# Zero matmuls in more of the early holes of the matrix engine, and exponentials of scores by one instruction a bank, in an attention and channel-mix kernel

## The chip, the core and the metric

The kernel runs on one core of a Trainium2 chip. Such a core has a matrix engine (TensorE, PE in the profile, with its weight loads as PEld), a vector engine (VectorE, DVE), a scalar engine for functions such as exp (ScalarE, ACT), a general engine (GpSimd, POOL) and an engine that issues transfers (SyncE, SP). Each works through its own instructions in order and waits for others by semaphores. TensorE writes its results into PSUM, eight banks of 512 float32 columns on 128 partitions. The metric is the device time in microseconds (us), smaller is better.

## What is computed

Attention with 32 memory slots for 8 batches of 8 heads, 576 tokens and 64 dimensions, then a channel mix of the RWKV kind (shift by one token, two projections, a squared ReLU, a gate):

```python
a = np.exp(phi - phi.max(2)); a = a / a.sum(2)
k_m, v_m = einsum('bhsm,bhsd->bhmd', a, k), einsum('bhsm,bhsd->bhmd', a, v)
attn = softmax(scale * q @ k_m.T)
x = (attn @ v_m), heads side by side: (8, 576, 512)
x_prev = x shifted by one token
xk, xr = mu_k * x + (1 - mu_k) * x_prev, mu_r * x + (1 - mu_r) * x_prev
k = np.maximum(xk @ w_k, 0); v = k * k @ w_v
out = sigmoid(xr @ w_r) * v
```

## The kernel before

The order of all work is written out by hand in `PLAN`, a list of words that is read once. A word `0:s0@0123` is a step of batch 0 (here the first part of its scores) that takes PSUM banks 0 to 3 for its results; `/a` and `/d` say which engine (ACT or DVE) does a step that either can do; `c0:6a` is a key product (the first part of the tokens for the seventh block of 128 columns of w_k), `g:` a gate, `o:` an output product, `r:` and `s:` ReLU and square, `p:` the issue of a load on POOL's queue, `b:8x8` eight matmuls on zeros of 8 x 64 = 512 columns. Since every engine keeps the order of its words, a word's place sets what it is queued behind.

Batches go through the same steps: exp of phi (line 298), sums over tokens (`z`, line 328) and products with k and v (`kg`, `vg`, `k`, `v`, `kv`, line 318), a transpose of the normalised k (`tk`, line 367), a transpose of q on DVE (`q0`, `q1`, lines 385 to 390), the scores (`s`, line 404), their exponentials on ACT (`es`, lines 420 and 425), the denominators, and the product of exponential and inverse denominator (`w`, in batch 0 `y`, line 466), which gives the attention weights.

Batch 0 goes its own way: denominators by matmul (`l`, line 432), logarithm and exponential on ACT (lines 437, 442), then `mk` and `mr` (line 361) mix tokens and values into x, `uk` and `ur` (line 547) copy it out as bf16, and the key products `c0:` (line 601) and gates (line 658) follow. The row mub (line 260) is a small product that spreads mu_k and mu_r. In batches 1 to 7 the values are folded into the weights first (`G`, line 493, copied out at line 499), and keys and gates are made from the attention weights (lines 619 to 679); their denominators come from DVE alone, which transposes the exponentials (`fe`, line 447), sums them (`fs`, line 453) and spreads the inverse (`fo`, line 459).

In batches 1 to 7 the tokens are kept with even ones before odd ones. The scores come out in another order, and the exponential writes them where they belong: for each of two halves of the batch (c) and two banks (w) four instructions (the four rows of `EVEN_ODD`, 5 or 4 blocks of 16 elements each, so 80 or 64 elements), 16 a batch. `weigh` then multiplies `e` and `lz` element by element into `at`, all three in the same order.

Matmuls on zeros: `keep_busy` writes into one tile, `idle`, in bank 7. `WARM` asks for 78 of 64 columns at the start; the words `b:` ask for 16 more, on 6720 columns, between `0:c10/a` and `0:s1@0123`, that is among the first steps of batch 0. `ps_tile` takes the next bank of a word, and its tile waits until the readers and writers of the tile that was there before are done; `covered` notes how many columns of a bank a tile has written.

Loads are issued by POOL in the order of the words `p:` (q, k, v, phi of later batches, and the weights wk, wr, wv), each waiting for earlier ones and for its buffer; phi and k of batch 0 are issued by ACT at the start.

Of the kernel before, what the change touches and what calls it, by code (L numbers as in the profile page):

```python
# [10 lines left out]
F32 = mybir.dt.float32  # L11
BF16 = mybir.dt.bfloat16
U32 = mybir.dt.uint32
AF = mybir.ActivationFunctionType
# [2 lines left out]


PLAN = [
# [71 lines left out]
NJ = 9  # L91
# [5 lines left out]
def kernel(  # L97
# [13 lines left out]
    nc = tc.nc  # L111
# [5 lines left out]
    scale = 1.0 / (D ** 0.5)  # L117
# [4 lines left out]
    PB = QR // 2  # L122
    HALVES = (slice(0, 5 * QR), slice(5 * QR, S))
    FIRST = (slice(0, 4 * QR), slice(4 * QR, S))
    CT = 512
# [11 lines left out]
    def ps_tile(shape, dtype, name, cover=0, onto=0):  # L137


        bank = next(now["banks"])  # L140
        if onto:
            assert covered.get(bank, 0) >= onto, (name, bank)
        else:
            covered[bank] = cover
        return psum.tile(shape, dtype, name=name, tag="ps" + bank, bufs=1)
# [31 lines left out]
    k0 = work.tile([128, HH, NJ, D], F32, name="k0f", tag="G", bufs=2)  # L177
# [55 lines left out]
    for g in range(4):  # L233
        r = slice(g * M, (g + 1) * M)
# [8 lines left out]
    xk_T, xr_T = x0_T[:, 0], x0_T[:, 1]  # L243
    sq = big.tile([128, NF, 2 * S], BF16, name="sq")

    idle = ps_tile([128, CT], F32, "idle")

    def keep_busy(n, blocks=CT // 64):
        for _ in range(n):
            ps = idle[:, :blocks * 64]  # L250
            nc.tensor.matmul(ps.rearrange("p (a b) -> p a b", b=64), lhsT=zeros,  # L251
                             rhs=zeros[:, :64].unsqueeze(1).to_broadcast([128, blocks, 64]), start=True, stop=True,
                             skip_group_check=True)

    keep_busy(*WARM)

    def load_mu_b():
# [9 lines left out]
    def load_mu():  # L267
# [2 lines left out]
        yield  # L270
        nc.vector.tensor_copy(mu1, ps_mu)

    EVEN_ODD = [(0, slice(0, 5), (0, slice(0, NJ, 2))), (0, slice(5, NJ), (1, slice(1, NJ, 2))),
                (1, slice(0, 4), (0, slice(1, NJ, 2))), (1, slice(4, NJ), (1, slice(0, NJ, 2)))]
    state = [{} for _ in range(B)]

    def scale_w(name):
# [11 lines left out]
    def attention(b):  # L289
        st = state[b]  # L290
# [119 lines left out]
        def exp_scores(c, js=slice(0, NJ)):  # L410

            def go():
                if "e" not in st:
                    st["e"] = work.tile([128, 2, S], BF16, name="e", tag="e", bufs=3)
                if b:
                    e = st["e"][:, c].rearrange("p (r v u) -> p r v u", r=2, u=PB)
                    for w in range(2):
                        ps = st["sc", 0][c, w].rearrange("p j (u r) -> p r j u", r=2)
                        for r, vs, js_ in EVEN_ODD:
                            nc.scalar.activation(e[:, r, vs, w * PB // 2:(w + 1) * PB // 2], ps[:, js_[0], js_[1]],  # L420
                                                 AF.Exp, scale=scale)
                    return
                e = st["e"][:, c].rearrange("p (j w t) -> p w j t", w=2, t=PB)
                for hf in range(2):
                    nc.scalar.activation(e[:, hf, js], st["sc", js.start][c, hf], AF.Exp, scale=scale)
            return go
# [35 lines left out]
        def weigh(c, sl=slice(0, S)):  # L462
            def go():
                if "at" not in st:
                    st["at"] = work.tile([128, 2, S], BF16, name="atn", tag="atn", bufs=3)
                nc.vector.tensor_mul(st["at"][:, c, sl], st["e"][:, c, sl], st["lz"][:, c, sl])  # L466
            return go

        def tr_v():
# [316 lines left out]
    for word in " ".join(PLAN).split():  # L786
        word, _, used = word.partition("@")
        word, _, now["by"] = word.partition("/")
        now["banks"] = iter(used)
        who, _, name = word.partition(":")  # L790
        if who == "p":
            preload(name)
        elif who == "b":
            keep_busy(*map(int, name.split("x")))
        else:
            queues[1:] = [nc.scalar] * (word in TAIL)
            parts = pending.pop(word, None) or (mixes[who][name] if who in mixes else attend[int(who)](name))()
            if hasattr(parts, "send") and next(parts, who) is not who:
                pending[word] = parts
# [31 lines left out]
```

## Time and profile before

| what | us |
|---|---|
| median of 3 runs (202.01 to 203.43) | 202.44 |
| the profiled execution's own time | 202.97 |
| its span, from the first instruction to the last | 201.0 |
| TensorE busy | 187.4 |
| VectorE busy | 158.8 |
| ScalarE busy | 152.3 |
| chain that ended last: TensorE, ScalarE, VectorE | 72%, 10%, 10% |

The profile is of one execution. Busy time of an engine is the union of its instructions. TensorE's matmuls overlap, and the end of each is modelled, so one of a group has a length that is longer than its share. In the rows of a timeline stand the start, the length, the engine, the line of the kernel, the operation, what it writes and reads, its shape, and the count of the instructions drawn together; in brackets the idle time of the engine before it and what ended it. "Clock" is the share of TensorE's full clock that was granted.

### The profile page before, as it was taken

Reading aid. Unit: us, or ns where it says so; the run is one execution under the profiler, and the core shown is the slowest. Engines: PE = TensorE matmul, PEld = TensorE weight load, DVE = VectorE, ACT = ScalarE, POOL = GpSimd, SP = SyncE. Lnnn points to the kernel's source line nnn. Section 1 sums busy time; section 2 is a strip of 40 time slices with the busy share of each in tenths; the row PEclk is TensorE's granted clock in tenths of the full one; section 3 lists DMA queues with packets and bytes.
Section 4 is the critical chain, followed back from the end, with each engine's and each line's share of the span. In section 5 each row is a group of like instructions: output and inputs, shape, how many; then the busy total and the mean of one; then the engine's idle time right before and its main releaser. Section 6 shows DMA issues by size and latency. Waiting matters only on the chain.

```text
span 201.0 us, 6598 instructions
## 1 busy us (share of the span) xinstructions
PE 187.4 (93%) x2650; PEld 106.4 (53%) x2650; DVE 158.8 (79%) x352; ACT 152.3 (76%) x434; POOL 29.3 (15%) x44
## 2 busy tenths in 40 slices
PE   8498798989999999999999999999999999999990
PEld 8334466548764455735655466346634564465440
DVE  2143479898887999999988999799979998999230
ACT  2427478988789688989899868998895799978310
POOL 7554320100170100502004200000000000000000
PEclk9999579999999999999999999999999999999997
DMA  5999999999999993599928999115102420123143
GB/s 195 278 203 265 206 208 199 253 220 283 225 171 214 208 308 120 94 231 287 293 74 126 213 248 245 31 40 137 36 3 65 118 82 10 47 76 86 33 124 104
DMA packets 26174, 31.95 MB, mean 159 GB/s; under 512 B 3096, under 2 KB 20768, under 8 KB 26144
## 3 DMA queue, kind: packets, MB, share of 16 engines
q0 software_dynamic: 17376, 20.32, 55.1%
q1 hardware_dynamic: 7408, 9.19, 15.9%
q10 hardware_dynamic: 1360, 2.03, 3.1%
q8 instruction: 20, 0.33, 0.6%
q14 instruction: 10, 0.08, 0.1%
HBM read 38.28 MB, written 9.44 MB: 237 GB/s over the span
## 4 chain that ended last, share of the span: by engine, by line
PE 72%; ACT 10%; DVE 10%; DMA 3%; issue 2%; ACTq 1%; DVEq 0%
PE pv L749 26%; PE pk L619 6%; PE pk L627 6%; PE pb L627 5%; PE gps L493 4%; PE pk L601 4%; PE kvps L318 3%; ACT e L420 3%; DMA k0f<-in_k_dram 3%; PE pr L679 3%; PE pr L671 2%; PE pb L679 2%; PE pv L743 2%; DVE rl L587 2%; ACT rl L585 2%; PE idle L251 2%
## 5 line engine op out<-in xcount | busy, mean ns | idle before, releaser
L749 PE MATMUL pv<-wv,sq 128*128 128x512 bf16 (+1 forms) x288 | 60.3, 356 | 0.3 <-DVE sq L593 0.2
L499 ACT CAST G<-gps 128x512 bf16<-128x512 f32 x75 | 40.5, 640 | 5.2 <-PE gps L493 4.9
L749 PEld LDWEIGHTS <-sq 128*128 128x128 bf16 x288 | 26.9, 97 | 29.3 <-issue 4.0
L755 DVE SCALAR_TENSOR_TENSOR o<-sg,pv 128x512 f32<-128x512 f32 (+3 forms) x41 | 24.4, 614 | 8.3 <-PE pv L749 5.0
L627 PEld LDWEIGHTS <-G 128*128 128x128 bf16 x224 | 21.3, 97 | 8.0 <-issue 1.0
L627 PE MATMUL pk<-diff,G 128*128 128x288 bf16 x112 | 22.9, 286 | 0.0
L627 PE MATMUL pb<-diff,G 128*128 128x288 bf16 x112 | 22.9, 286 | 0.0
L593 DVE TENSOR_TENSOR sq<-rl 128x576 bf16<-128x576 bf16 (+2 forms) x49 | 20.6, 438 | 1.8 <-ACT rl L585 0.7
L623 ACT COPY pb<-pk 128x288 f32<-128x288 f32 x43 | 16.6, 398 | 5.7 <-PE pk L619 4.0
L619 PE MATMUL pk<-atn,G 128*128 128x288 bf16 x112 | 20.3, 286 | 0.0
L585 ACT ACTIVATE rl<-pk 128x288 bf16<-128x288 f32 (+2 forms) x39 | 16.2, 419 | 3.8 <-PE pk L627 2.0
L648 ACT ACTIVATE sg<-pr 128x512 f32<-128x512 f32 x22 | 13.5, 624 | 7.2 <-PE pr L701 4.0
L585 ACT ACTIVATE rl<-pb 128x288 bf16<-128x288 f32 x36 | 14.7, 424 | 3.5 <-PE pb L627 3.3
L587 DVE TENSOR_SCALAR rl<-pk 128x288 bf16<-128x288 f32 (+2 forms) x33 | 14.5, 447 | 1.5 <-PE pk L601 1.0
L420 ACT ACTIVATE e<-scps 128x80 bf16<-128x80 f32 (+1 forms) x112 | 15.0, 320 | 0.1
L502 DVE TENSOR_TENSOR G<-G 128x1024 bf16<-128x1024 bf16 x21 | 14.1, 683 | 0.5 <-ACT G L499 0.4
L466 DVE TENSOR_TENSOR atn<-e,lz 128x576 bf16<-128x576 bf16 (+2 forms) x18 | 12.1, 688 | 3.0 <-ACT lz L442 2.8
L619 PEld LDWEIGHTS <-G 128*128 128x128 bf16 x112 | 10.6, 98 | 5.5
L591 ACT ACTIVATE sq<-rl 128x576 bf16<-128x576 bf16 (+2 forms) x23 | 12.4, 561 | 0.4 <-DVE rl L587 0.3
L298 ACT ACTIVATE em<-ph 128x1152 bf16<-128x1152 f32 (+1 forms) x9 | 9.8, 1083 | 1.8 <-DMA ph<-in_phi_dram 1.8
L601 PE MATMUL pk<-x0T,wk 128*128 128x256 bf16 (+1 forms) x64 | 10.9, 326 | 0.0
L251 PE MATMUL idle<-zeros 128*128 128x64 bf16 (+3 forms) x94 | 9.7, 280 | 1.0 <-DVE zeros L180 1.0
(100 smaller groups left out, 285.4 us busy)
## 6 DMA issues: line engine op xcount, KB each, us to landing
out_dram<-o SPq DMA_DIRECT2D x134, 64.0 KB, 3.5
ph<-in_phi_dram POOLq DMA_DIRECT2D x7, 576.0 KB, 10.3
kv<-in_k_dram POOLq DMA_DIRECT2D x7, 576.0 KB, 13.6
q<-in_q_dram POOLq DMA_DIRECT2D x7, 576.0 KB, 12.7
kv<-in_v_dram POOLq DMA_DIRECT2D x7, 576.0 KB, 13.1
k0f<-in_k_dram ACTq DMA_DIRECT2D x2, 576.0 KB, 6.9
wv<-in_moe_w_v_dram POOLq DMA_DIRECT2D x2, 512.0 KB, 19.1
ph<-in_phi_dram ACTq DMA_DIRECT2D x1, 576.0 KB, 4.6
```

Source lines behind the costliest of these rows:

```text
L420: nc.scalar.activation(e[:, r, vs, w * PB // 2:(w + 1) * PB // 2], ps[:, js_[0], js_[1]], AF.Exp, scale=scale)
L499: return lambda: copier()(g_tile()[:, v, c, GCOLS[i]], st["gps", v, i][c])
L502: return lambda: nc.vector.tensor_sub(g_tile()[:, 1, :, GCOLS[i]], g_tile()[:, 2, :, GCOLS[i]], g_tile()[:, 0, :, GCOLS[i]])
L585: nc.scalar.activation(rl, ps, AF.Relu, scale=HALF ** 0.5)
L587: nc.vector.tensor_scalar(rl, ps, 0.0, HALF ** 0.5, op0=AL.max, op1=AL.mult)
L593: nc.vector.tensor_mul(dst, rl, rl)
L601: nc.tensor.matmul(pk, lhsT=wk_sb[:, di, fi * 128:(fi + 1) * 128], rhs=xk_T[:, di, sl], start=(di == 0), stop=(di == ND - 1))
L619: nc.tensor.matmul(pa, lhsT=st["G"][:, 2, c, f], rhs=st["at"][:, c, :NP], start=c == 0, stop=False, skip_group_check=True)
L623: copier()(pb, pa)
L627: nc.tensor.matmul(ps, lhsT=st["G"][:, v, c, f], rhs=st["d"][:, kind, c], start=False, stop=c == 1, skip_group_check=True)
L749: nc.tensor.matmul(pv[:, cols], lhsT=sq[:, fi, lo:lo + 128], rhs=wv_sb[:, fi, cols], start=(fi == 0), stop=(fi == NF - 1))
L755: nc.vector.scalar_tensor_tensor(o[:, cols], in0=gated[name][:, cols], scalar=1.0, in1=pv[:, cols], op0=AL.add, op1=AL.mult)
```

## The change

There are two parts, and the rest of the order stays: without the words `b:`, the two plans are the same, word for word.

1. The words `b:` are now 42 matmuls on 18816 columns in place of 16 on 6720. They stand from the first exponential of phi to the key products of batch 0 (the last before `c0:2a`), most in bank 7, some in banks 3, 6 and 2. `keep_busy` takes a tile of its own for each word, in the bank that the word names, and so waits for that bank's last readers and writers. The 78 at the start stay.
2. The exponentials of batches 1 to 7 are one instruction for each bank, of 288 elements, that writes even and odd tokens of each block apart (4 a batch in place of 16); the order of blocks that `EVEN_ODD` made is now made by `weigh`, whose product reads `e` and `lz` in the order of blocks and writes `at` even before odd.

```diff
-    "0:exp0 0:c01/d 0:c00/a 0:exp1 0:z@0 0:z 0:mub@1 0:mub p:q:0h 0:kg0@02 0:c11/d 0:q1 0:c10/a b:8x8 b:1x2 0:kg1",
-    "0:h1/a 0:h0/a b:2x8 b:1x5 0:tk@0 0:q0 p:v:0h p:v:0g 0:tk b:1x8 b:1x4 0:s0@0123 0:es00 0:vg1@45 0:es10 b:1x3",
-    "0:l00@6 0:l00 b:1x3 0:s1@0123 0:l10@6 0:es11 p:wk:0-2 0:r00 0:y00 0:vg0 0:mu@2 0:mu 0:l10 0:l11@7 p:wk:4-8",
-    "0:es01 p:wk:2-4 0:l01@0 p:phi:1 0:nk0 0:nk1 0:r10 0:y10 0:l01 0:mk0@2130 0:l11 0:nr1 p:k:1 p:q:1 0:r01 0:r11",
+    "0:exp0 0:c01/d 0:c00/a 0:exp1 b:7x8@7 b:1x5@7 0:z@0 0:z 0:mub@1 0:mub p:q:0h 0:kg0@02 0:c11/d 0:q1 0:c10/a",
+    "b:10x8@7 0:kg1 0:h1/a 0:h0/a b:3x8@7 b:1x4@7 0:tk@0 0:q0 p:v:0h p:v:0g 0:tk b:2x8@7 0:s0@0123 0:es00 b:1x4@7",
+    "0:vg1@45 0:es10 b:1x7@7 0:l00@6 0:l00 b:1x6@7 0:s1@0123 b:1x4@7 0:l10@6 0:es11 p:wk:0-2 0:r00 0:y00 0:vg0",
+    "b:1x4@3 0:mu@2 0:mu 0:l10 0:l11@7 p:wk:4-8 0:es01 p:wk:2-4 b:1x8@3 b:1x8@6 0:l01@0 p:phi:1 0:nk0 0:nk1 0:r10",
+    "0:y10 0:l01 b:3x8@6 b:1x4@6 0:mk0@2130 0:l11 0:nr1 p:k:1 p:q:1 0:r01 0:r11 0:nr0 0:y01 0:y11 b:3x8@6 0:mk1@4576",
+    "0:uk01/a 0:uk00/a c0:6a@0 c0:5a@1 0:uk11/d 0:uk10/a 0:mr0@2347 0:ur01/d b:1x4@6 c0:6b@5 c0:3b@6 c0:4b@3 c0:0a@7",
...
+    "0:ur11/a p:wv:0-2 c0:5a/d b:1x4@6 1:z@6 c0:2b@7 c0:3b/d c0:0a/a b:1x4@2 c0:3a@4 c0:7a@5 c0:5b/d 0:tb c0:6a/a",
+    "0:ur10/d 1:k@12 c0:3a/a m:k0/d c0:5b/d b:1x4@3 c0:2a@3 1:z 1:nk/d c0:6a/a c0:1b@6 c0:7b@1 c0:3a/a c0:7b/a",
...
-    idle = ps_tile([128, CT], F32, "idle")
-
     def keep_busy(n, blocks=CT // 64):
+        ps = ps_tile([128, CT], F32, "idle", cover=blocks * 64)[:, :blocks * 64]
         for _ in range(n):
-            ps = idle[:, :blocks * 64]
             nc.tensor.matmul(ps.rearrange("p (a b) -> p a b", b=64), lhsT=zeros,
...
-                    e = st["e"][:, c].rearrange("p (r v u) -> p r v u", r=2, u=PB)
+                    e = st["e"][:, c].rearrange("p (h j u) -> p h j u", h=2, u=PB)
                     for w in range(2):
-                        ps = st["sc", 0][c, w].rearrange("p j (u r) -> p r j u", r=2)
-                        for r, vs, js_ in EVEN_ODD:
-                            nc.scalar.activation(e[:, r, vs, w * PB // 2:(w + 1) * PB // 2], ps[:, js_[0], js_[1]],
-                                                 AF.Exp, scale=scale)
+                        nc.scalar.activation(e[:, :, :, w * PB // 2:(w + 1) * PB // 2],
+                                             st["sc", 0][c, w].rearrange("p j (u h) -> p h j u", h=2), AF.Exp, scale=scale)
...
-                nc.vector.tensor_mul(st["at"][:, c, sl], st["e"][:, c, sl], st["lz"][:, c, sl])
+                out, e, z = st["at"][:, c, sl], st["e"][:, c, sl], st["lz"][:, c, sl]
+                if b:
+                    out = out.rearrange("p (r v u) -> p v r u", r=2, u=PB)
+                    e, z = (x.rearrange("p (v r u) -> p v r u", r=2, u=PB) for x in (e, z))
+                nc.vector.tensor_mul(out, e, z)
```

More of the change, by code (lines that the diff above doesn't have):

```diff
@@ L271, in load_mu @@
         nc.vector.tensor_copy(mu1, ps_mu)
-    EVEN_ODD = [(0, slice(0, 5), (0, slice(0, NJ, 2))), (0, slice(5, NJ), (1, slice(1, NJ, 2))),
-                (1, slice(0, 4), (0, slice(1, NJ, 2))), (1, slice(4, NJ), (1, slice(0, NJ, 2)))]
     state = [{} for _ in range(B)]
```

5 rows, old and new, of the table PLAN are left out of this document.

## The prediction

> **What bounds the kernel now.** I read the page first (whole span, then the 40 slices), then the clock by stretches, then TensorE's timeline, and last what the other engines and the loads do beside it.
>
> ```profile
> span 201.0 us, 6598 instructions
> PE 187.4 (93%) x2650; PEld 106.4 (53%) x2650; DVE 158.8 (79%) x352; ACT 152.3 (76%) x434; POOL 29.3 (15%) x44
> PE   8498798989999999999999999999999999999990
> PEclk9999579999999999999999999999999999999997
> ```
>
> TensorE (PE) is busy in nine tenths or more of every slice from about 40 us to the end: there the kernel is bound by TensorE. Only the first 40 us (eight slices) have holes and a lower clock. In stretches (us from the start, then busy time by engine, granted clock, DMA share, GB/s):
>
> ```profile
> 8.50:13.68 5.18, 5.18 (x53) 2.63 (x50) 2.85 (x8) 0.67 (x1) 2.23 (x3) 1.00 1.23 214
> 13.68:20.51 6.83, 5.75 (x212) 3.05 (x210) 2.30 (x9) 4.79 (x18) 3.26 (x4) 1.00 1.26 249
> 20.51:27.34 6.83, 5.81 (x65) 3.24 (x66) 3.43 (x11) 3.72 (x12) 2.01 (x3) 0.50 1.22 207
> 27.34:32.00 4.66, 4.66 (x133) 3.44 (x131) 3.98 (x13) 4.17 (x8) 0.99 (x2) 1.00 1.27 203
> ```
>
> From 20.51 to 27.34 half the clock was granted, after a stretch with 1.08 us of holes. The 1.00 before 13.68 cannot be taken at its word, as TensorE's timeline shows (start, length, then the group):
>
> ```profile
> 0.99 4.34 PE L251 MATMUL idle<-zeros 128*128 128x64 bf16 x78 [0.99 <-DVE zeros L180]
> 8.20 0.40 PE L328 MATMUL zps<-ones,em 128*128 128x2 bf16 x9 [2.86 <-ACT em L298]
> 8.52 1.21 PE L260 MATMUL mub<-mu,sel 8*128 8x128 f32 x4
> 9.67 0.67 PE L318 MATMUL kvps<-kv,em 64*32 64x64 bf16 x36
> 10.27 3.63 PE L251 MATMUL idle<-zeros 128*128 128x512 bf16 x9
> 13.82 0.45 PE L318 MATMUL kvps<-kv,em 64*32 64x64 bf16 x36
> 14.21 0.74 PE L251 MATMUL idle<-zeros 128*128 128x512 bf16 x3
> 15.06 0.28 PE L367 MATMUL ktps<-identity,kbd 128*128 128x128 bf16 x2
> ...
> 20.96 0.43 PE L361 MATMUL mxps<-atn,vm 32*64 32x256 bf16 x4 [0.48 <-DVE atn L466]
> 21.96 0.75 PE L361 MATMUL mxps<-atn,vm 32*64 32x256 bf16 x20 [0.57 <-issue]
> 22.64 1.89 PE L601 MATMUL pk<-x0T,wk 128*128 128x256 bf16 x8
> 24.45 0.65 PE L361 MATMUL mxps<-atn,vm 32*64 32x256 bf16 x24
> 25.04 3.89 PE L601 MATMUL pk<-x0T,wk 128*128 128x320 bf16 x20
> 28.86 0.48 PE L361 MATMUL mxps<-atn,vm 32*64 32x256 bf16 x24
> ...
> 33.48 1.04 PE L601 MATMUL pk<-x0T,wk 128*128 128x256 bf16 x8
> 35.21 0.48 PE L404 MATMUL scps<-qT,kmT 32*32 32x288 bf16 x32 [0.69 <-DVE qT L385]
> ```
>
> The same eight matmuls of 256 columns take 1.89 us at 22.64 (clock 0.50) and 1.04 at 33.48 (clock 1.00): 0.85 us more for 2048 columns, so about 0.42 ns a column at full clock and 0.83 at half. The fillers at 10.27 (eight of 512 and one of 128 columns, 4224) take 3.5 us up to 13.82: 0.83 ns a column, so half clock. Those at 14.21 (1344 columns, 0.74 us with the last one's tail) ran at full clock. So the clock was at half from the start until about 13.7, and rose after a stretch (10.27 to 13.65) that zeros alone had filled.
>
> **The fillers before 15 us.** The seven of 512 and one of 320 columns (3904) stand in the hole from 5.33 to 8.20. At half clock they take 3.24 us and end 0.4 late, at full clock 1.64. TensorE is then without a hole from 0.99 on, which by the rise at 13.7 (some 3.4 us of full work) is enough: I take the clock as full from 5 to 7 us, so that z (8.20) is late by nothing to 0.4 us. After z, the four matmuls of mub save 0.4 us (estimate: half of their columns' time) and kvps 0.22 (0.67 against 0.45), so the next filler starts near 9.65 instead of 10.27. It is longer, 5120 columns, but takes 2.15 us and ends at 11.8. Its real successor, the second kvps group, waits for casts of k:
>
> ```profile
> 9.84 0.67 ACT L303 CAST kv<-k0f 128x576 bf16<-128x576 f32 x1 [1.70 <-DMA k0f<-in_k_dram]
> 20.64 1.20 ACT L547 CAST x0T<-mxps 128x256 bf16<-128x256 f32 x4
> 35.77 2.08 ACT L420 ACTIVATE e<-scps 128x80 bf16<-128x80 f32 x16
> 55.15 0.71 ACT L585 ACTIVATE rl<-pb 128x288 bf16<-128x288 f32 x2 [0.20 <-PE pb L627]
> 55.75 0.42 ACT L585 ACTIVATE rl<-pk 128x288 bf16<-128x288 f32 x1
> 10.45 0.45 DVE L303 CAST kv<-k0f 128x576 bf16<-128x576 f32 x1
> 27.99 0.49 DVE L587 TENSOR_SCALAR rl<-pk 128x320 bf16<-128x320 f32 x1 [0.98 <-PE pk L601]
> 35.39 1.41 DVE L286 TENSOR_SCALAR mwr<-wr,mu 128x512 bf16<-128x512 bf16 x4
> 37.88 0.78 DVE L447 STREAM_TRANSPOSE eT<-e 128x576 uint32<-128x576 uint32 x1 [0.69 <-ACT e L420]
> ```
>
> Both casts (ACT and DVE) are done by 10.9, so the filler ended last at 13.82 and ends last still at 11.8: **gain 2.0**. The bounds are 0.7 (clock full only from about 10.3, filler from 10.9 to 13.1) and 2.9 (casts alone).
>
> [...]
>
> **From 15 to 22 us.** The fillers here (up to 1792 columns, 0.75 us at full clock) lie in holes while ACT works through exponentials and logarithms and DVE through products. Several wait for a bank's reader (banks 3 and 6: ACT's exponential or logarithm), each of which the work behind them needs or has ended by then. The longest, before mk0, may end 0.2 late; the one before mk1 (1536 columns, 0.64 us) ends about when DVE's last product does. TensorE's next real work, the first key matmuls (22.64), needs ACT's casts (20.64 and 1.20, so 21.84, moved to 19.8) and mk1 (0.75, about 0.5 at full clock). It starts near 20.05: 2.6 early, 0.6 of it new.
>
> **From 22 to 30 us, the clock.** If the holes are filled the clock stays. Rows 22.64 and 33.48 give 0.85; rows 24.45 and 28.86 give 0.17; the 2.30 us from 25.04 to 27.34 ran at half and become 1.15. That is 2.17, less 0.1 for 256 new columns: **2.0 more, 4.6 in all**. Who is next late? DVE had waited 0.98 us for these results at 27.99, and its work before that, which follows the matmuls at 24.45, moves by 2.6 + 0.85 + 0.17 = 3.6, so it too arrives 4.6 early and has no slack left. From there to 35.21 DVE is the bound, and hands the 4.6 on. Three further fillers of 256 columns (banks 6, 2, 3) cost 0.1 each; that on bank 2 waits for DVE's evacuation of 5b, with the key matmuls of 3a and 7a queued behind it: up to 0.2.
>
> **The loads** could take this back:
>
> ```profile
> 12.79 0.74 POOL L201 DMA_DIRECT2D wr<-in_moe_w_r_dram  x1 [0.66 <-DMA kv<-in_v_dram]
> wr<-in_moe_w_r_dram POOLq DMA_DIRECT2D x1, 512.0 KB, 16.2
> ```
>
> The DMA share stays above 1 in all stretches, so loads don't come earlier. wr lands at 12.79 + 16.2 = 29.0; its reader (35.39) moves to 30.8: 1.8 us to spare. POOL's issue order does not change.
>
> ```profile
> L466 DVE TENSOR_TENSOR atn<-e,lz 128x576 bf16<-128x576 bf16 (+2 forms) x18 | 12.1, 688 | 3.0 <-ACT lz L442 2.8
> ```
>
> **The exponentials**, and the product behind them (above). For each of batches 1 to 7, 16 instructions become 4 of 288 elements. The 16 take 2.08. Two of 288 (line 585, at 55.15) take 0.71 and one 0.42, so each further one costs 0.29 and four take 1.29: 0.79 less. At 37.88 DVE waits 0.69 for exactly this: **0.7 gained in batch 1**. In the six others TensorE hardly stops (the page's slices), so the gain lies between 0 and 6 x 0.79 = 4.7; I take 0.15 each, 0.9, near zero since TensorE is the bound. The product (line 466) writes what the exponentials used to permute: as many elements of the same types, so taken as 0; the ends are 0 and its whole time again (0.69 us for each of 14), which DVE's 21% of idle time would not hide. Nearest is 0: no data is added.
>
> [...]
>
> **Sum.** 4.6 + 0.7 + 0.9 = 6.2, less 0.3 for fillers that end late: 5.9. The profiled execution took 202.97 (span 201.0 and 1.97 around it) and becomes 197.1; the median of the runs shown, 202.44, is 0.5 lower: **196.5 us**.
>
> **Rivals.**
> - *Cold fillers outlast the holes* (slower). If the clock does not rise before 13.7, the first fillers delay z by 0.4, the 5120 columns take 4.25 instead of 3.5 us (+0.7), and where the clock falls again at 20.5 those from 19 us on add about 1 us; four or five of 256 columns add 0.2 each. That is +3.0, less 1.6 from the exponentials: **203.9**, and above 205 if these give nothing. It decides where TensorE is not at full clock by about 10 us. For it: half clock until 13.7 despite 78 fillers at the start. Against: these left a hole of 2.9 us that is now filled. [...] Chance 6%, and 1% for the product at its upper end.
> - *The clock falls at 20.5 all the same*, because fillers do not make up for small matmuls of 32 rows: 2.0 early and 1.6 from exponentials, less the 1.9 of cold fillers from 19 us on: **200.7**. For it: even in 13.68 to 20.51 TensorE was 84% busy. Chance 7%.
> - *DVE or loads hold the middle*: the gain at the first key matmuls (2.6) stays, the clock's 2.0 is lost in DVE's queue between 28 and 35 us, 0.7 from exponentials: **199.1**. For it: DVE is 4.0 of 4.66 us busy from 27.34. Against: its own waits of 0.98. Chance 17%.
> - *The exponentials free TensorE later too*, 0.5 a batch: **194.4**. Chance 9%.
>
> **Numbers.** The forecast has the remaining 60%, with its own range 195.3 to 198.0. The range of 194.2 to 200.0 takes in the third and fourth rivals and the forecast's bounds, and leaves out the first two with 0.14. One per cent (2 us) is about what a measurement here tells from no change; the runs shown spread over 1.4 us. Faster by over 1% (below 200.4): forecast, third, fourth, 0.86; within 1%: the second, 0.07; slower: the first, with the product's upper end, 0.07.
>
> **What would show it.** In the changed profile: the 512-column fillers after 9 us start some 215 ns apart rather than 427; granted clock 1.00 from 20 to 27 us; the second kvps group near 11.8, the first key matmuls near 20, scores of batch 1 near 30.6, four exponentials in 1.3 us; TensorE gapless from about 40. It is wrong if z or kvps waits on a filler at half clock, or if the scores of batch 1 are less than 3 us early.

## The result and the profile after

| | median, us | ratio to before, 95% interval |
|---|---|---|
| before (19 runs) | 203.39 | |
| after (19 runs) | 201.39 | 0.992 (0.989 to 0.994) |

The change is worth 1.7 us, 0.8%, where 5.9 had been forecast; the time lies outside the range. The profiled execution took 201.73 us (202.97 before).

The page of the kernel after, its span, TensorE's share, and the 40 slices of TensorE and of the granted clock:

```profile
span 199.8 us, 6543 instructions
...
PE 185.4 (93%) x2655; PEld 105.9 (53%) x2676; DVE 159.6 (80%) x352; ACT 147.0 (74%) x350; POOL 29.3 (15%) x44
...
PE   8797999999999999799999999999999999999950
...
PEclk9999999999999999999999999999999999999996
```

The clock row no longer has its dip at 20 to 27 us: what the fillers were to do, they did. But TensorE has a 7 in the 17th slice (80 to 85 us) that was a 9 before, and the last two slices, 5 and 0, were 9 and 0. These are two places with which the prediction did not deal. TensorE's timeline of the kernel after, with the rows that answer to those of before, and the second of these places at its end:

```profile
8.09 0.38 PE L325 MATMUL zps<-ones,em 128*128 128x2 bf16 x9 [0.91 <-ACT em L295]
8.40 0.71 PE L259 MATMUL mub<-mu,sel 8*128 8x128 f32 x4
9.04 0.45 PE L315 MATMUL kvps<-kv,em 64*32 64x64 bf16 x36
9.42 2.33 PE L250 MATMUL idle<-zeros 128*128 128x512 bf16 x10
11.68 0.45 PE L315 MATMUL kvps<-kv,em 64*32 64x64 bf16 x36
...
18.56 0.38 PE L358 MATMUL mxps<-atn,vm 32*64 32x256 bf16 x10
20.15 0.31 PE L358 MATMUL mxps<-atn,vm 32*64 32x192 bf16 x14 [1.22 <-issue]
20.40 0.82 PE L250 MATMUL idle<-zeros 128*128 128x512 bf16 x3
21.15 0.60 PE L358 MATMUL mxps<-atn,vm 32*64 32x256 bf16 x24
21.68 1.05 PE L600 MATMUL pk<-x0T,wk 128*128 128x256 bf16 x8
...
25.84 0.48 PE L358 MATMUL mxps<-atn,vm 32*64 32x256 bf16 x24
...
32.32 0.56 PE L401 MATMUL scps<-qT,kmT 32*32 32x288 bf16 x32 [0.20 <-DVE qT L382]
...
80.03 0.46 PE L401 MATMUL scps<-qT,kmT 32*32 32x288 bf16 x25
81.63 0.32 PE L401 MATMUL scps<-qT,kmT 32*32 32x288 bf16 x7 [1.14 <-issue]
```

Twice TensorE stops in the middle of a group, in mk0 at 18.9 (ten matmuls done, fourteen to come) and in batch 3's scores at 80.5, and the releaser is "issue": it waited for no engine and no transfer that the profile knows. How far the same matmul is moved, from the two timelines:

| place | before | after | earlier by | forecast |
|---|---|---|---|---|
| second kvps group | 13.82 | 11.68 | 2.1 | 2.0 |
| first key matmuls | 22.64 | 21.68 | 1.0 | 2.6 |
| mixing group behind the slow clock | 28.86 | 25.84 | 3.0 | 4.6 |
| scores of batch 1 | 35.21 | 32.32 | 2.9 | 4.6 |
| output product, 64 us | 63.68 | 60.20 | 3.5 | |
| folded values of batch 3, 88 us | 88.41 | 86.29 | 2.1 | |
| last gate | 192.53 | 189.86 | 2.7 | |
| end of the span | 201.0 | 199.8 | 1.2 | 5.9 |

So there are three losses: 1.6 us before 22, 1.4 at 81, and 1.5 behind the last gate. The third shows in what SP waits for over the last 12 us, first of the kernel before, then of the kernel after (us in total, times, longest):

```profile
SPq L732 <- DVE o L755: 5.1, 2, 5.0
SPq L732 <- DMA out_dram<-o: 1.6, 1, 1.6
```

```profile
SPq L731 <- DMA out_dram<-o: 3.2, 2, 1.6
```

SP issues the last stores. After the change it waits twice in place of once for an earlier store to land.

**What "issue" is.** Section 3 of the page has a queue of kind "instruction". Before, then after (packets, MB, share):

```profile
q8 instruction: 20, 0.33, 0.6%
```

```profile
q8 instruction: 21, 0.34, 0.7%
```

0.34 MB in 21 packets are 16 KB each. I counted TensorE's instructions in program order, weight loads and matmuls alike (5295 before, 5347 after: 26 more matmuls with a weight load each; the weight loads of either trace, taken twice, are five more). The stop in mk0 lies between the instructions 695 and 696, that in the scores between 2740 and 2741: 2045 apart, eight times 256 less three. The three are waits on semaphores, which are instructions of TensorE too but not in the count; the trace has them at 52.04, 76.12 and 77.39 us. With such waits counted, all 17 stops in the table under Experiments come at the same remainder of 256. So a packet is a block of 256 instructions, of 64 bytes each by this count, and the stops stand at the borders of blocks. In the kernel before the stop lies between 694 and 695, which falls in mk1, and there stands the row "21.96 ... [0.57 <-issue]", which the prediction quoted and passed over. The times of the packets in the trace give the mechanism. The block that begins at 440 was entered at 14.30 us (16.11 before), the next packet began at 17.90 (19.59) and took 0.94 (0.89), and instruction 696 ran 1.31 (1.48) after it had landed: 5.85 us from entry to entry (5.86). TensorE had done its 256 instructions in 4.4 us, and stood still.

At most borders no such stop shows: of the 21 packets of the kernel after, two have one of 0.3 us or more ahead of the block that they bring, of the 20 of the kernel before one.

Theory A, then: the change added 26 matmuls, moved the borders of the blocks onto dense stretches of small matmuls, and pays there. Theory B: the number of instructions plays no part; the fillers' columns, banks and waits, or DVE's queue, take the gain back.

### The profile page after: what moved, and what is told of

Its sections match the earlier page's. It is cut to its first block, busy times and chain, and to the rows that moved or that the text cites. A ratio compares the mean times of both kernels' runs of the same rounds, so it can differ in the third digit from the quotient of the medians.

```text
span 199.8 us, 6543 instructions
## 1 busy us (share of the span) xinstructions
PE 185.4 (93%) x2655; PEld 105.9 (53%) x2676; DVE 159.6 (80%) x352; ACT 147.0 (74%) x350; POOL 29.3 (15%) x44
## 4 chain that ended last, share of the span: by engine, by line
PE 77%; DVE 7%; ACT 4%; DMA 3%; issue 3%; SPq 1%; ACTq 1%; DVEq 0%
PE pv L748 25%; PE pk L618 7%; PE pk L626 6%; PE pb L626 6%; PE gps L492 5%; PE idle L250 4%; PE kvps L315 3%; PE pv L742 3%; PE pk L600 3%; DMA k0f<-in_k_dram 3%; PE pb L678 3%; PE pr L670 2%; PE pr L678 2%; DVE rl L586 2%; ACT G L498 2%
## 5 line engine op out<-in xcount | busy, mean ns | idle before, releaser
L748 PE MATMUL pv<-wv,sq 128*128 128x512 bf16 (+1 forms) x276 | 59.3, 355 | 1.1 <-issue 0.5
L498 ACT CAST G<-gps 128x512 bf16<-128x512 f32 x75 | 39.5, 620 | 7.6 <-PE gps L492 7.4
L250 PE MATMUL idle<-zeros 128*128 128x64 bf16 (+3 forms) x120 | 15.2, 277 | 1.2 <-DVE zeros L181 1.0
L382 DVE STREAM_TRANSPOSE qT<-q 128x576 uint32<-128x576 uint32 x14 | 10.6, 766 | 0.0
L415 ACT ACTIVATE e<-scps 128x288 bf16<-128x288 f32 x28 | 9.4, 424 | 1.4 <-PE scps L401 1.4
```

Source lines behind the costliest of these rows:

```text
L498: return lambda: copier()(g_tile()[:, v, c, GCOLS[i]], st["gps", v, i][c])
L748: nc.tensor.matmul(pv[:, cols], lhsT=sq[:, fi, lo:lo + 128], rhs=wv_sb[:, fi, cols], start=(fi == 0), stop=(fi == NF - 1))
```

## Experiments

The 78 matmuls of 64 columns at the start are a lever: they run in a hole, before any data is there, so their number can be changed without touching the work, and each one moves all later borders by two instructions. Each kernel's own runs of before stood beside it (medians 202.71, 203.01 and 203.28 us in the three series), so ratios are compared. The whole table first; "stops" are TensorE's waits on "issue" of 0.3 us and more in the trace, and the last column is the time from the start of the last gate matmuls to the end of the span.

| kernel | TensorE instructions | median, us | ratio (95%) | stops, us | packets | last gate to end |
|---|---|---|---|---|---|---|
| before | 5295 | | 1 | mk1 0.6 | 20 | 8.5 |
| after | 5347 | 201.39 | 0.992 (0.989 to 0.994) | mk0 1.2, scores of batch 3 1.1 | 21 | 9.9 |
| after, start 39 x 128 | 5269 | 198.65 | 0.981 (0.976 to 0.985) | mk1 0.9 | 20 | 8.5 |
| after, start 13 x 384 | 5217 | 200.29 | 0.987 (0.983 to 0.992) | scores of batch 0 1.3, k products of batch 3 1.2 | 20 | 8.5 |
| exponentials alone | 5295 | 201.37 | 0.993 (0.990 to 0.996) | mk1 0.8 | 20 | 8.5 |
| fillers alone | 5347 | 202.69 | 1.001 (0.998 to 1.005) | mk0 1.5, scores of batch 3 0.3 | 21 | 9.9 |
| after, start 52 x 96 | 5295 | 198.58 | 0.977 (0.972 to 0.982) | mk1 0.6 | 20 | 8.4 |
| after, start 110 x 45 | 5411 | 202.49 | 0.997 (0.993 to 1.000) | k products of batch 0 1.4, transposes of batch 3 1.3 | 21 | 10.1 |
| before, start 104 x 48 | 5347 | 205.26 | 1.011 (1.007 to 1.014) | mk0 2.3, scores of batch 3 0.6 | 21 | 10.0 |
| 52 x 96, no late fillers | 5287 | 198.21 | 0.975 (0.970 to 0.981) | mk1 0.6 | 20 | 8.4 |
| fillers alone, start 52 x 96 | 5295 | 200.07 | 0.986 (0.981 to 0.991) | k products of batch 0 0.3, mk1 0.6 | 20 | 8.5 |
| before, start 52 x 96 | 5243 | 201.50 | 0.992 (0.989 to 0.995) | none | 20 | 8.5 |

**Fewer instructions at the start.** In the kernel after:

```diff
-WARM = (78, 1)
+WARM = (39, 2)
```

that is 39 matmuls of 128 columns, the same 4992 columns.

> The changed kernel with its start fillers as 39 matmuls of 128 columns in place of 78 of 64: the same columns, 78 fewer instructions of TensorE (a weight load and a matmul each). Theory A (TensorE's program arrives in blocks of 16 KB, 256 instructions; TensorE stops where it reaches a block before its transfer has landed): all block borders move 78 instructions later in the work. The stop of 1.2 us in the mixing matmuls of batch 0 and that of 1.1 us in the scores of batch 3 shrink to under 0.9 us together, the 21st transfer of 16 KB disappears from the last stores (the time from the last output product to the end falls from 6.3 to 4.8 us): about 3 us under the changed kernel, near 198.5. Theory B (the stops are waits for a bank or for another engine, and belong to the work): they stay at the same matmuls, and the time stays within 0.5 us of the changed kernel.

A further step, `WARM = (13, 6)`:

> The changed kernel with its start fillers as 13 matmuls of 384 columns: the same columns again, 130 fewer instructions. Theory A: the borders now fall where TensorE issues many short matmuls between two of them (scores and mixing of batch 0, 15 to 28 us, and the products with k and v of batches 3 and 4 near 76 us): the stops grow to some 6 to 9 us in sum, less 1.5 us at the end, where no 21st transfer falls: 2 to 5 us over the changed kernel, 203 to 206. Theory B: within 0.5 us of the changed kernel.

The first came as A had it, if somewhat short: some 2.3 us faster than after by the ratios, where about 3 had been expected. The stop in batch 3's scores is gone, and one of 0.95 is left, in mk1, where under 0.9 had been expected. The second was to be slower than after and was faster, by 1.0 us. Its trace has the two stops that follow from the count, and no other:

```profile
15.45 0.32 PE L401 MATMUL scps<-qT,kmT 32*32 32x128 bf16 x27
17.05 0.24 PE L401 MATMUL scps<-qT,kmT 32*32 32x128 bf16 x5 [1.29 <-issue]
...
79.60 0.36 PE L315 MATMUL kvps<-kv,em 64*32 64x128 bf16 x24 [1.25 <-issue]
```

The first of them lies between the instructions 440 and 441, five matmuls before the end of a group that in the kernel after ran without a break; 440 is 696 less 256. What failed was the size: I had put every block at 5.85 us or more behind the one before it, but this one was entered 5.2 behind, and that at 79.6 us 3.0 behind. And the longer end was gone.

**Each part alone.** The kernel before with the new exponentials and product, and the kernel after with the old ones:

```diff
-                        for r, vs, js_ in EVEN_ODD:
-                            nc.scalar.activation(e[:, r, vs, w * PB // 2:(w + 1) * PB // 2], ps[:, js_[0], js_[1]],
-                                                 AF.Exp, scale=scale)
+                        nc.scalar.activation(e[:, :, :, w * PB // 2:(w + 1) * PB // 2],
+                                             st["sc", 0][c, w].rearrange("p j (u h) -> p h j u", h=2), AF.Exp, scale=scale)
```

> The kernel before with the second part of the change alone: exponentials by one instruction a bank, the product writing the permuted order. TensorE's program is that of before, so by theory A its stops stay as before and only the exponentials count: 0.5 to 0.7 us at batch 1 and 0 to 0.9 later, so 0.5 to 1.6 us under before. If the permuted product cost VectorE more, the time would be over before.

> The changed kernel with the exponentials and the product of before: the fillers alone. TensorE's program is that of the changed kernel. Theory A: the same stops near 19 and 80 us and the same late transfer, 0.5 to 1.5 us over the changed kernel, so between 0 and 1.5 us under before, though the clock is full from about 5 us on. Theory B expects the same of this run; the run prices the part.

The exponentials alone gain 1.4 us (0.8 to 2.1; 0.5 to 1.6 was expected), so nearly the whole of the change's gain; the fillers alone nothing (from 1.0 slower to 0.5 faster; 0 to 1.5 faster was expected).

**The same zeros, another number of instructions.** The start again, with the same columns to within 1%, and on both kernels:

```diff
-    keep_busy(*WARM)
+    warm = ps_tile([128, CT], F32, "idle", cover=96)[:, :96]
+    for _ in range(52):
+        nc.tensor.matmul(warm, lhsT=zeros, rhs=zeros[:, :96], start=True, stop=True, skip_group_check=True)
```

In the kernel after this takes away as many matmuls as the fillers add:

> The changed kernel with its 78 start matmuls of 64 columns as 52 of 96: the same 4992 columns on zeros, 26 matmuls (52 instructions) fewer, so 5295 instructions on TensorE as before the change. Theory A (TensorE's program comes in blocks of 256 instructions, and a block cannot be entered sooner than some 5.8 us, later some 4 us, after the one before): the stop in batch 3's scores near 81 us goes (-1.4), the stops before 22 us come to about 1.0 in two places in place of 1.5 in one, the 21st packet of instructions at the end goes and with it the longer tail (-1.5): 198.4 us, 197.6 to 199.3. Theory B (the number of instructions plays no part, the losses are those of the fillers' columns and of DVE): as the changed kernel, 201.4.

198.58: as A expected. With 110 matmuls of 45 columns:

> The changed kernel with its 78 start matmuls of 64 columns as 110 of 45: about the same columns (4950), 32 matmuls (64 instructions) more. Theory A: the border of the third block falls in the scores of batch 0 near 16 us, 3 us before the block can be there; stops before 22 us near 3.5 in place of 1.5, another of 0.5 to 1.2 near 33 us, the one near 82 us stays between 1 and 2: 204.2 us, 202.6 to 205.6. Theory B: as the changed kernel, 201.4.

Slower than after by 1.0 us (0.5%; the intervals overlap a little), less than A's 1.2 to 4.2. Two borders made the stops, the first again inside a group of small matmuls:

```profile
16.10 0.36 PE L317 MATMUL kvps<-kv,em 64*32 64x64 bf16 x24
17.88 0.27 PE L317 MATMUL kvps<-kv,em 64*32 64x64 bf16 x12 [1.42 <-issue]
...
82.25 0.22 PE L366 MATMUL ktps<-identity,kbd 128*128 128x128 bf16 x1 [1.34 <-issue]
```

The early stop is where it was expected (near 16 us), but took 1.4 where 3 was expected, since its packet came 1.7 us after the entry to the block and not 3.6; the one near 33 us did not come. What came, unexpected, is a stretch at half the clock behind the stop:

```profile
18.52:21.93 3.41, 3.35 (x32) 1.27 (x32) 2.36 (x8) 1.27 (x4) 1.83 (x3) 0.50 1.17 268
```

In the kernel after the granted clock was 1.00 there. The first key matmuls start at 23.33, 1.65 later than in the kernel after, though the stops before them take nearly the same (1.42 and 1.22). So the 1.0 us is not the price of the stops alone. That the stop let the clock fall is likely by its place, but not shown. The 21st packet began 1.2 us after the start of the last gate, in the kernel after 2.3, and the loss lies earlier too: ACT was held 1.98 us in the issue of a store while the packet was under way, TensorE waited 1.83 us for ACT's last sigmoid in place of 0.28, and SP waited once for 3.2 in place of twice for 1.6.

The sharpest test is the kernel before with 104 start matmuls of 48 columns: not one column more, only the fillers' 26 instructions.

> The kernel before with its 78 start matmuls of 64 columns as 104 of 48: the same 4992 columns, 26 matmuls more and nothing else, so 5347 instructions as in the changed kernel. Theory A: a stop appears in batch 3's scores near 84 us (0.6 to 1.4), the stop in mk1 near 22 us moves to mk0 (first key matmuls 0 to 0.4 later), a 21st packet of instructions appears shortly before the end and the time from the last output product to the end grows from 4.8 to about 6.3: 2.0 to 3.2 slower than before, about 205.5 us. Theory B: as before, within 0.5 us.

2.2 us slower than before (1.5 to 2.8), by the three moves expected. In the trace, the stop in mk0 and that in batch 3's scores:

```profile
22.16 1.18 PE L362 MATMUL mxps<-atn,vm 32*64 32x256 bf16 x46 [2.27 <-issue]
```

```profile
85.53 0.32 PE L405 MATMUL scps<-qT,kmT 32*32 32x288 bf16 x8 [0.61 <-issue]
```

and, at the end, SP's doubled wait:

```profile
SPq L733 <- DMA out_dram<-o: 3.3, 2, 1.7
```

Only the early size was off: the stop hit mk0 two matmuls in, not ten, and the first key matmuls came at 23.83, 1.2 late in place of 0 to 0.4.

**The late fillers.** The kernel with 52 start matmuls, without the four words behind the first key matmuls:

```diff
-    "0:uk01/a 0:uk00/a c0:6a@0 c0:5a@1 0:uk11/d 0:uk10/a 0:mr0@2347 0:ur01/d b:1x4@6 c0:6b@5 c0:3b@6 c0:4b@3 c0:0a@7",
+    "0:uk01/a 0:uk00/a c0:6a@0 c0:5a@1 0:uk11/d 0:uk10/a 0:mr0@2347 0:ur01/d c0:6b@5 c0:3b@6 c0:4b@3 c0:0a@7",
```

and so for `b:1x4@6` before `1:z`, `b:1x4@2`, and `b:1x4@3` before `c0:2a`.

> As the changed kernel with 52 start matmuls of 96 columns, and without its four fillers of 256 columns behind the first key matmuls (in banks 6, 6, 2 and 3). These took TensorE 0.6 us later at 34 us than at 29 us in the trace, where it had key products to do: 0.4 to 0.6 faster than with them, 197.9 us. If they hold the clock at full speed or hide waits, no gain, or slower by up to 1 us.

The median is 0.4 lower, but the intervals lie over each other, so it isn't settled. The trace has both: the four cost nothing any more, and the scores of batch 1 wait 0.7 us for DVE's transposed q again, where 0.2 had been left.

**Fillers alone, at the old number; and the old number reduced.** The start of 52 x 96 on the kernel with the fillers alone, and on the kernel before:

> The fillers of the change alone (exponentials and product as before), with the 78 start matmuls of 64 columns as 52 of 96, so with 5295 instructions on TensorE as before the change. Theory A: the fillers with 26 instructions more gained nothing; at an equal number they keep what they win, without the stop in batch 3's scores (0.6 there), the longer tail (1.5) and half of the stop in mk0: 2.5 to 3.5 faster than before, 199.9 us. Theory B (fillers cannot gain here, whatever their number): as before, within 0.7.

> The kernel before with its 78 start matmuls of 64 columns as 52 of 96, 26 fewer and nothing else: 5243 instructions. Theory A: the border that stopped mk1 at 21 us now falls in the key matmuls, 6 us or more behind the border before it, so that stop goes and the first key matmuls start 0.7 to 1.0 earlier, near 21.8; near 80 us another border falls into the products with k of batch 3, under 2 us behind the one before it, and TensorE stops there for 1.0 to 1.5. Together within 0.7 of before, but by two moves that the trace shows. Theory B: the stop of 0.57 in mk1 stays where it is, and nothing happens near 80 us.

The first gave 2.8 us (1.8 to 3.8) where the same fillers had given nothing with 52 instructions more: A's 2.5 to 3.5. The second gave 1.6, more than expected, since only half of A's story came. The stop in mk1 is gone, and the wait that it hid is bare:

```profile
21.24 0.94 PE L362 MATMUL mxps<-atn,vm 32*64 32x256 bf16 x24 [0.48 <-DVE atn L467]
22.12 1.89 PE L602 MATMUL pk<-x0T,wk 128*128 128x256 bf16 x8
...
24.52 3.09 PE L602 MATMUL pk<-x0T,wk 128*128 128x320 bf16 x20
```

The key matmuls start 0.5 earlier (0.7 to 1.0 was expected). A further 0.8 is the clock's and not the count's: in this trace half the clock was granted from 21.77 to 25.18, in that of the kernel before from 20.51 to 27.34, and the twenty key matmuls take 3.09 us in place of 3.89. From 34 us on 1.1 of this is left. How much of the 1.6 us over all executions is the clock's stays open. But the stop near 80 us did not come: TensorE passed that border 1.9 us behind the one before. Its packet had begun at 77.03, 1.2 us ahead of the entry to the block (78.24), while in the kernel after the one at 78.44 began 1.2 behind it. TensorE had been 15.6 us in the block before, 9.1 in the other. So what counted here was not the time between borders but when the next packet began, and behind the slower of the two blocks it began early. What decides that moment, which in the kernel after alone ranged from 2.5 before the entry to a block to 4.4 after it, these runs don't tell.

## Why the prediction was wrong

*The early fillers, 2.0 us*: right. The second kvps group starts 2.1 earlier, and the bounds of 0.7 and 2.9 did not come to bear: in the eight profiled kernels with the fillers the group started between 11.30 and 11.85. The granted clock rose at 4.69 us in the trace of the kernel after (its start matmuls of 64 columns begin 53 ns apart before that, 29 behind it) and at 6.73 in another, in all eight before z, which comes near 8, so where it rose made no difference to the gain; that it could rise only at 10.3, on which the 0.7 rests, no run shows. Nor is 3.4 us of full work shown to be enough: in the kernel before 4.34 us of start matmuls brought no rise, in the kernel after it came 3.70 us into them.

*The clock, 2.0 us*: right. TensorE's busy time and granted clock after the change, from 20.51 us, where half was granted before:

```profile
20.51:27.34 6.83, 6.77 (x118) 4.39 (x117) 4.99 (x15) 6.03 (x16) 2.21 (x3) 1.00 1.22 208
```

Between the first key matmuls and the mixing group at 28.86 the kernel gains 2.06 us. No cold filler, no fallen clock: the first two rivals had no part in this execution, though the time lies near that of the second. It is not so in all executions. Four of the 19 had a granted clock of 0.978 to 0.986 over the whole and spans of 200.3 to 201.4 us, the other fifteen 0.989 to 0.996 and 198.3 to 200.0. Where those four lost the clock no trace shows, nor that small matmuls of 32 rows take it away.

*"It starts near 20.05"*: this step failed. The sum let the first key matmuls follow ACT's casts and mk1, and took the row with "0.57 <-issue" for ordinary work. They started at 21.68. In mk0 the eleventh matmul started 1.46 us after the tenth, and 21.68 less 1.46 is 20.2: the working was right for a TensorE that never waits for its own program. The next block came 5.85 us after the one before, as in the kernel before; the faster TensorE was through with its 256 instructions, the longer it stood. Of the 2.6 forecast, 1.5 went there.

*The fillers were costed at their columns and holes alone*, 0.3 us. What was overlooked is that an instruction had a cost far from its place: 26 matmuls more before 36 us moved a border into batch 3's scores at 80 us (1.4) and brought a 21st packet at 192 us, among the last stores, with the end 1.5 us longer. That the number of instructions does it, not the fillers, is shown: the same number without the fillers costs the kernel before 2.2 us, and the fillers at the old number gain 2.8. A longer end goes with the packet throughout: all four kernels with 21 packets before the end take 9.9 to 10.1 us from the last gate, the eight with 20 take 8.4 to 8.5. How one packet (1.31 us, from 192.12, in the kernel after) holds back the stores is not shown.

*The exponentials*: right in sum, 1.4 us alone against 1.6. ACT's row and the product's, of the kernel after:

```profile
33.21 1.29 ACT L415 ACTIVATE e<-scps 128x288 bf16<-128x288 f32 x4
```

```profile
L465 DVE TENSOR_TENSOR atn<-e,lz 128x576 bf16<-128x576 bf16 (+2 forms) x18 | 12.1, 689 | 3.3 <-ACT lz L437 3.1
```

1.29 us for four, as worked out, and 689 ns for a product against 688; these means mix shapes, and the 14 products of batches 1 to 7 alone take 755 ns against 754 (not 0.69 us, as the prediction has it). Only the share of batch 1 was smaller than 0.7 and that of the later ones larger: from 42 to 192 us the kernel after gains 0.5 and 0.6 more, apart from the stop.

*The late fillers*: from 28.86 to 34 us TensorE fell back by 0.6 us, not 0.3. That is part of why the step around batch 1 gave -0.1, where 0.7 less 0.3 had been forecast.

Added up, in us: 1.0 to the first key matmuls, 2.1 by the clock, -0.1 around batch 1, 1.1 by the later exponentials, -1.4 by the stop at 81 and -1.5 at the end make the 1.2 of the span. The rival that DVE or the loads hold the middle, put at 17%, would have shown as waits of TensorE on DVE in the stage from 24 to 34 us; there is one, of 0.20.

The best version measured is the change with fewer, wider matmuls at the start and without the late fillers: 0.975 of the time before (0.970 to 0.981). The wider matmuls alone, on the kernel before, give as much as the whole change did, if in part by the clock.

## What to carry to other kernels

Where an engine waits in the middle of a group of its own small instructions and the profile names "issue", count its instructions. Here all 17 such stops lay at the same remainder of 256, and TensorE was waiting for its own program: work made faster ahead of it left the block at 5.85 us behind the one before and made the stop longer (0.57 us before, 1.22 after), and 26 matmuls more moved it. Filler work in fewer and wider instructions had fewer borders (20 packets with 52 start matmuls, 21 with 78), but where they fall counts as well: the start as 13 matmuls of 384 columns was slower here than as 39 of 128 or 52 of 96. A change that adds instructions is compared with one that adds none by changing the number of some that do nothing. A gain counted early in a long kernel isn't in hand until its later borders and its end have been looked at.

## What the runs showed that was not expected

A border's price runs from nothing to 2.3 us (mk0 in the kernel before with 104 matmuls at its start). A packet of 16 KB took 0.88 us (the one at 161.88 us of the kernel before) to 1.72 (that at 78.44 of the kernel after), and where TensorE was waiting for one it went on 1.31 and 1.47 us after it had landed (after), 1.48 (before). The kernel before stood still at such a border too, by 0.6 us, and 26 start matmuls fewer, with the same columns, made it 0.8% faster (0.5% to 1.1%), in part by the clock.
